# Last output tile in two column pieces, and split value and sum columns for eight attention pairs in place of four

## The chip, the cores and the metric

The kernel runs on one core of a Trainium2 chip. The metric is the device time of one execution in microseconds (us), given as the median of several executions. "The span" is the time from the first to the last instruction in one profiled execution; it lies some 1.7 us below the device time.

## The reference

Attention with a short "beacon" in front of the keys, causal, on 8 batches of 8 heads; then a dense MLP on its output.

```python
# q, k, v: (8, 8, 576, 64)   beacon_k, beacon_v: (8, 8, 16, 64)
k_all = concatenate([beacon_k, k], axis=2)
v_all = concatenate([beacon_v, v], axis=2)
scores = q @ k_all^T / sqrt(64);  scores[future keys] = -1e9
a = exp(scores - max);  a /= a.sum(-1) + 1e-9
x = (a @ v_all) as (4608 tokens, 512)
h = x @ w_in                                  # 512 -> 2048
out = (h * sigmoid(1.702 h)) @ w_out          # 2048 -> 512, float32
```

## The kernel before

The attention is done in 32 steps; a step is a "pair" of heads of one batch. TensorE makes the scores, ACT their exponentials, GpSimd and DVE the causal mask, and then TensorE multiplies the exponentials by an array that holds the values and, beside them, columns of a constant; those columns give the sums by which the values are divided. Tokens of finished pairs go through the MLP in nine groups of 512, whose matmuls are threaded between the pairs. So TensorE nearly always has work.

There are two forms for values and sums. The **old form** makes one tile per head and half, with the values on 64 partitions and the sums on the other 64. It is evicted from PSUM to an SBUF tile `O`, and all later work reads that copy:

```python
def av_half(i, x, half):                       # head x of pair i: 7 matmuls for two halves
    u = psu.tile([P, AQ[half + 1] - AQ[half]], F32, tag="u", name="u")
    ...
        nc.tensor.matmul(u[:, lo:hi], vb[...128 columns: values and constant...], E[0:kw, x, ...], ...)
def av_out(i, x, half, eng):                   # eviction, on DVE or ACT
    copy[eng](out=Os[i][:, x, AQ[half] : AQ[half + 1]], in_=avu[(i, x, half)][:, :])
def z_turn(i, x):                              # sums: transpose 32x32 squares
    nc.vector.transpose(zst[i][0][64*x : 64*x+64, :, :], Os[i][64*(1-x) : 64*(1-x)+64, x, :])
# z_recip: 1/sum;  z_back: transpose back;
def norm(i, x, eng):                           # values * 1/sum, 64 partitions
    vec[eng].tensor_tensor(out=xT[r : r+64, ...], in0=Os[i][r : r+64, x, :], in1=zst[i][2][r : r+64, :], op=ALU.mult)
```

The **split form** sends values (z = 0) and sums (z = 1) of both heads to tiles of their own, with the two heads side by side in two 64-column parts of the array. Both are read straight from PSUM; the pair's two sum tiles are made first, then its two value tiles:

```python
def av_both(i, half, z):                       # 32 matmuls a pair
    u = psu.tile([P, AQC[half + 1] - AQC[half]], F32, tag="u", name="u")
    ...
            for x in range(2):
                nc.tensor.matmul(u[64*x : 64*x+64, lo:hi], vb[0:kw, j, 2*p + x, z*D : (z+1)*D], Es[i][0:kw, x, ...], ...)
def z_turn_both(i, half):
    nc.vector.transpose(zst[i][0][:, ...], avu[(i, half, 1)][:, :])
def norm_both(i, half):
    nc.vector.tensor_tensor(out=xT[:, p, ...], in0=avu[(i, half, 0)][:, :], in1=zst[i][2][:, qa:qe], op=ALU.mult)
```

All these tiles, and those of the MLP, come from one ring of four PSUM buffers called "u" (`rings = dict(..., u=4, ...)`). The second layer of the MLP and its store:

```python
def mlp2(g, mt):                               # 16 matmuls of 512 columns
    o = psu.tile([P, DMODEL], F32, tag="u", name="u")
    for nt in range(NNT):
        nc.tensor.matmul(o[:, :], gts[g][:, nt, mt*P : (mt+1)*P], w2t[:, nt, :], ...)
def mlp2_out(g, mt, eng): ...                  # copy o to SBUF "osb" on DVE or ACT
def mlp2_store(g, mt):
    nc.sync.dma_start(out=out[t0 : t0 + P, :], in_=ou[(g, mt)][:, :])
```

The order of all instructions is chosen while the program is built, by a list scheduler in the kernel. Every piece of work has a duration (the "price"), things it needs, and perhaps a buffer. The scheduler takes the piece that can start first by its own clock, and emits it. Each engine then runs its own list in order, waiting where it must.

```python
while todo:
    for w in todo:
        t = 0.0
        for n in w.needs: ...; t = max(t, n.t1 + SEM)         # everything it needs is done
        if w.alloc is not None: ...                            # the buffer's former users are done
        eng = min(w.opts, key=lambda e: max(t, free[e]) + w.opts[e] + BIAS[t > 45].get(e, 0))
        c = (t, 0 if w.mode == mode == 1 else 1, w.key)
        ...                                                    # the smallest c wins
    w.t0 = t; w.t1 = t + d; free[eng] = t + d
    if w.dma:
        if eng == "POOL":                                      # loads that GpSimd issues
            f = max(dma_free["POOL"], t + d + 1.6) + w.dma
            w.t1 = f + (0.4 if t < 40 else 1.0)                # believed landing
```

The softmax here doesn't subtract the row's maximum and nothing guards it: scores larger than these inputs give would overflow.

Of the kernel before, what the change touches and what calls it, by code (L numbers as in the profile page):

```python
# [10 lines left out]
F32 = mybir.dt.float32  # L11
# [5 lines left out]
def kernel(  # L17
# [11 lines left out]
    nc = tc.nc  # L29
# [5 lines left out]
    DMODEL = H * D  # L35
    DFF = moe_w_in.shape[1]
    P = 128
# [5 lines left out]
    NNT = DFF // P  # L43
# [8 lines left out]
    GT = 512  # L52
    NG = NTOK // GT
# [15 lines left out]
    sp = ctx.enter_context(tc.tile_pool(name="sp", bufs=3))  # L69
    pss = ctx.enter_context(tc.tile_pool(name="pss", bufs=2, space=bass.MemoryType.PSUM))  # L70
    psu = ctx.enter_context(tc.tile_pool(name="psu", bufs=4, space=bass.MemoryType.PSUM))
    dr = ctx.enter_context(tc.tile_pool(name="dr", bufs=4, space=bass.MemoryType.DRAM))

    copy = dict(ACT=nc.scalar.copy, DVE=nc.vector.tensor_copy, POOL=nc.gpsimd.tensor_copy)
# [20 lines left out]
    w2t = cst.tile([P, NNT, DMODEL], F16, tag="w2", name="w2")  # L95
# [435 lines left out]

    ou = {}

    def mlp2(g, mt):
        o = psu.tile([P, DMODEL], F32, tag="u", name="u")
        ou[(g, mt)] = o
        for nt in range(NNT):
            nc.tensor.matmul(  # L538
                o[:, :],
                gts[g][:, nt, mt * P : (mt + 1) * P],  # L540
                w2t[:, nt, :],
                start=(nt == 0),
                stop=(nt == NNT - 1),
            )

    def mlp2_out(g, mt, eng):
        osb = sp.tile([P, DMODEL], F32, tag="osb", name="osb")
        if eng == "ACT":
            nc.scalar.copy(out=osb[:, :], in_=ou[(g, mt)][:, :])
        else:  # L550
            nc.vector.tensor_copy(out=osb[:, :], in_=ou[(g, mt)][:, :])  # L551
        ou[(g, mt)] = osb

    def mlp2_store(g, mt):
        t0 = g * GT + mt * P
        nc.sync.dma_start(out=out[t0 : t0 + P, :], in_=ou[(g, mt)][:, :])



# [21 lines left out]
    )  # L581
    SEM, QS = 0.1, 0.1
    SPL, CAP = 2.0, 2.0
    NBOTH = 4
    HWQ = 3

    def use(buf, *ws):
# [3 lines left out]
    Lq, V, W1, W2 = {}, {}, [], []  # L591
# [81 lines left out]
    for b in range(B):  # L673
# [5 lines left out]
        for g in range(2) if b >= NB2 else ():  # L679
            for w in (1, 0):  # L680
                k0 = 4 * b + 2 * g - 2.5 + 0.2 * (1 - w)
# [3 lines left out]
                    dma=1.4,  # L685
# [12 lines left out]
                for e in range(2):  # L698
# [3 lines left out]
                        tr, alloc=tb_ if e == 0 else None, after=cp[:1],  # L702
# [3 lines left out]
                if w == 1:  # L706
                    if bkB is None:
# [3 lines left out]
                                alloc=stb["bk"] if x == 0 else None, dma=0.2,  # L711
# [9 lines left out]
                        bkB, after=cp[:1],  # L721
# [4 lines left out]
                    dma=0.9,  # L726
# [4 lines left out]
                    alloc=bt[w] if g == 0 else None, dma=1.2,  # L731
                    after=[placed[(b, 0, w)]] if g == 1 else (),
# [4 lines left out]
        for j in range(NJ):  # L737
            V[(b, j)] = Work(
                "POOL", 0.88 + 0.54 * (j == 0), kv + 0.1 * j, lambda b=b, j=j: load_v(b, j),
                alloc=vbb[b] if j == 0 else None, after=[V[(b, 0)]] if j else (),  # L740
                dma=1.1 + 0.1 * (j == 0),
            )
    for c in range(4):
# [3 lines left out]
            after=[Lq[(2, 1, 0)]],  # L747
# [20 lines left out]
    for i in range(NSTEP):  # L768
# [5 lines left out]
        for c in range(len(CH)):  # L774
# [6 lines left out]
                alloc=s_, mode=1,  # L781
# [8 lines left out]
                alloc=Eb if c == 0 else None,  # L790
                after=[first] if first else exps[i - 1][:1] if i else (),
# [16 lines left out]
        if i < NBOTH:  # L808
            for z in (1, 0):
                for half in range(2):  # L810
# [8 lines left out]
                        after=avs[-1:],  # L819
# [5 lines left out]
                    if z == 1:  # L825
# [3 lines left out]
                            alloc=zb[0] if not zn else None, after=zn[:1],  # L829
                        ))  # L830
                        use(ub[(half, 1)], zn[-1])
        else:
            Ob = Buf("O")
            evs = []
            for x in range(2):
                for half in range(2):
                    mm = av_list(x, half)
                    u_ = Buf("u")
# [14 lines left out]
                        alloc=Ob if not evs else None, after=evs[:1],  # L853
# [4 lines left out]
                    alloc=zb[0] if not zn else None, after=zn[:1],  # L858
# [5 lines left out]
        if i < NBOTH:  # L864
            for half in range(2):
# [3 lines left out]
                    after=[norms[b * NPAIR][0]] if p + half else (),  # L869
# [27 lines left out]
    m1s, m2s = {}, {}  # L897
    for g in range(NG):
        gb[g] = Buf("g")
        bs = range(g * GT // S, ((g + 1) * GT - 1) // S + 1)  # L900
        gl = []
        k0 = ends[g] - 1 + 2 * max(0, g - 7)
        for n in range(NNT):
            u_ = Buf("u")
            m = Work(
                "PE", 0.88, k0 + 0.05 * n, lambda g=g, n=n: mlp1(g, n),
                [x for b in bs for p in range(NPAIR) for x in norms[b * NPAIR + p]] + [W1[n // 4]],
                alloc=u_,
            )
            m1s.setdefault(g, []).append(m)  # L910
            for b in bs:
                use(xTb[b], m)
            gl.append(Work(
                "ACT", 0.6 + (LOAD if n == 0 else 0), k0 + 0.05 * n - 0.3,
                lambda g=g, n=n: mlp1_gelu(g, n), [m], alloc=gb[g] if n == 0 else None,
                after=gl[:1] if n else exps[ends[g] - 1] + prev,
            ))
            use(u_, gl[-1])
        if ends[g] < NSTEP:
            x = exps[ends[g]][0]  # L920
            x.opts = dict(ACT=x.opts["ACT"] + LOAD)
            x.after += gl
        prev = gl
        for n in range(GT // P):
            u_, o_ = Buf("u"), Buf("osb")
            k1 = k0 + 1 + n
            m = Work("PE", 3.46, k1, lambda g=g, n=n: mlp2(g, n), gl + W2, alloc=u_)
            m2s[(g, n)] = m
            use(gb[g], m)
            oc = Work(  # L930
                dict(ACT=0.6, DVE=0.66), 0, k1 - 0.3, lambda eng, g=g, n=n: mlp2_out(g, n, eng),
                [m], alloc=o_,
            )
            use(u_, oc)
            ot = Work("SP", 0.73, k1, lambda g=g, n=n: mlp2_store(g, n), [oc], dma=0.9)
            use(o_, ot)


# [139 lines left out]
```

## Time and profile before

| | before |
|---|---|
| device time, median of 3 runs | 367.96 us (367.85 to 367.99) |
| span of the profiled run | 366.9 us (that execution took 368.57 us) |
| busy: PE, DVE, ACT, POOL (GpSimd) | 353.5, 249.3, 228.0, 153.1 us |
| first matmul of MLP group 0 | 35.54 us |
| starts of group 0's output tiles | 59.42, 65.91, 71.95, 77.95 us |
| last matmul's end, last copy's start | 363.18, 363.20 us |

TensorE (PE) is busy for 96% of the span, so what counts is where it waits. In the timelines a row is: start, length, engine, line of the kernel, operation, out<-in, shapes, how many instructions, and in brackets the idle time before the row with what ended it. A row without brackets followed what was before it closely.

### The profile page before, as it was taken

Reading aid. Unit: us, or ns where it says so; the run is one execution under the profiler, and the core shown is the slowest. Engines: PE = TensorE matmul, PEld = TensorE weight load, DVE = VectorE, ACT = ScalarE, POOL = GpSimd, SP = SyncE. Lnnn points to the kernel's source line nnn. Section 1 sums busy time; section 2 is a strip of 40 time slices with the busy share of each in tenths; the row PEclk is TensorE's granted clock in tenths of the full one; section 3 lists DMA queues with packets and bytes.
Section 4 is the critical chain, followed back from the end, with each engine's and each line's share of the span. In section 5 each row is a group of like instructions: output and inputs, shape, how many; then the busy total and the mean of one; then the engine's idle time right before and its main releaser. Section 6 shows DMA issues by size and latency. Waiting matters only on the chain.

```text
span 366.9 us, 6133 instructions
## 1 busy us (share of the span) xinstructions
PE 353.5 (96%) x2349; PEld 176.8 (48%) x2349; DVE 249.3 (68%) x421; ACT 228.0 (62%) x335; POOL 153.1 (42%) x264
## 2 busy tenths in 40 slices
PE   7689999999999999999999999999999999999995
PEld 3355444444444444544445864544444454444442
DVE  5547499999999986999599949981995183010021
ACT  4669787648765776677857675677658734616200
POOL 9678567593368245743376236710430010000000
PEclk9969999999999999999999999999999999999999
DMA  9999999994689645894479537921100011000012
GB/s 143 148 206 189 188 237 234 220 113 100 191 235 175 129 130 145 129 171 132 126 111 142 164 112 144 134 88 32 59 30 29 2 57 57 2 29 29 30 57 86
DMA packets 69788, 43.41 MB, mean 118 GB/s; under 512 B 42624, under 2 KB 62080, under 8 KB 69760
## 3 DMA queue, kind: packets, MB, share of 16 engines
q0 software_dynamic: 49152, 18.19, 48.6%
q1 hardware_dynamic: 20400, 24.55, 21.2%
q8 instruction: 18, 0.29, 0.3%
q10 hardware_dynamic: 208, 0.29, 0.3%
q14 instruction: 10, 0.08, 0.1%
HBM read 44.60 MB, written 16.61 MB: 167 GB/s over the span
## 4 chain that ended last, share of the span: by engine, by line
PE 79%; DVE 11%; DMA 3%; ACT 3%; POOL 2%; issue 1%; DVEq 0%; POOLq 0%
PE u L516 34%; PE u L538 30%; PE u L401 7%; PE s L331 6%; DMA g<-in_q_dram 3%; ACT E L344 2%; DVE zt L470 2%; DVE O L459 2%; DVE xT L489 2%; DVE t L262 1%; PE u L430 1%; POOL vb L221 1%; DVE rz L480 1%; DVE osb L551 1%; PE u L190 1%
## 5 line engine op out<-in xcount | busy, mean ns | idle before, releaser
L344 ACT ACTIVATE E<-s 128x1024 f16<-128x1024 f32 (+3 forms) x128 | 103.4, 865 | 48.7 <-PE s L331 46.5
L538 PE MATMUL u<-w,g 128*128 128x512 f16 x576 | 129.2, 379 | 0.6 <-DVE O L459 0.4
L516 PE MATMUL u<-xT,w 128*128 128x512 f16 (+1 forms) x640 | 126.0, 358 | 0.0
L528 ACT ACTIVATE g<-u 128x512 f16<-128x512 f32 x144 | 85.2, 597 | 42.8 <-PE u L516 42.5
L367 POOL TENSOR_SCALAR_AFFINE_SELECT E<-E 128x256 f16<-128x256 f16 (+2 forms) x148 | 63.8, 450 | 83.8 <-ACT E L344 83.6
L516 PEld LDWEIGHTS <-w 128*128 128x128 f16 x640 | 62.1, 98 | 61.3 <-issue 0.9
L538 PEld LDWEIGHTS <-g 128*128 128x128 f16 x576 | 54.5, 98 | 65.4 <-issue 3.6
L551 DVE COPY osb<-u 128x512 f32<-128x512 f32 x30 | 20.5, 683 | 65.2 <-PE u L538 65.0
L459 DVE COPY O<-u 128x240 f32<-128x240 f32 (+1 forms) x84 | 34.8, 440 | 24.4 <-PE u L401 22.1
L262 POOL COPY t<-sq 128x576 f16<-128x576 f16 x21 | 26.7, 1274 | 49.2 <-DVE sq L253 42.8
L401 PE MATMUL u<-E,vb 128*128 128x240 f16 x392 | 46.8, 266 | 0.2
L489 DVE TENSOR_TENSOR xT<-O,rz 64x576 f16<-64x576 f32 x56 | 44.3, 790 | 0.8
L470 DVE STREAM_TRANSPOSE zt<-O 64x576 f32<-64x576 f32 x56 | 43.1, 770 | 1.4
L401 PEld LDWEIGHTS <-vb 128*128 128x128 f16 x392 | 32.2, 98 | 17.4 <-issue 8.0
L331 PE MATMUL s<-qT,kT 64*128 64x80 f16 (+5 forms) x384 | 37.1, 285 | 2.8 <-ACT E L344 1.8
L253 DVE STREAM_TRANSPOSE sq<-n 128x576 f16<-128x576 f16 x48 | 34.9, 747 | 6.6 <-DMA n<-in_k_dram 6.3
L221 POOL DMA_DIRECT2D vb<-in_v_dram x40 | 34.4, 866 | 3.6 <-DMA w<-in_moe_w_in_dram 2.6
L262 DVE COPY t<-sq 128x576 f16<-128x576 f16 x27 | 27.6, 1021 | 0.3
L331 PEld LDWEIGHTS <-kT 64*128 64x128 f16 x384 | 13.3, 94 | 27.4 <-issue 19.4
L480 DVE STREAM_TRANSPOSE rz<-rt 128x576 f32<-128x576 f32 x32 | 24.4, 763 | 0.6
L459 ACT COPY O<-u 128x336 f32<-128x336 f32 (+1 forms) x28 | 10.7, 428 | 2.9 <-PE u L401 2.7
L1043 PE MATMUL u<-wu 128*128 128x512 f16 x29 | 10.5, 456 | 1.3 <-DVE wu L1036 1.3
(44 smaller groups left out, 124.5 us busy)
## 6 DMA issues: line engine op xcount, KB each, us to landing
out_dram<-osb SPq DMA_DIRECT2D x36, 256.0 KB, 2.1
d<-t SPq DMA_DIRECT2D x12, 296.0 KB, 2.6
kT<-d SPq DMA_DIRECT2D x12, 296.0 KB, 3.4
n<-in_k_dram POOLq DMA_DIRECT2D x12, 288.0 KB, 4.8
n<-in_q_dram POOLq DMA_DIRECT2D x12, 288.0 KB, 5.9
d<-t SPq DMA_DIRECT2D x12, 288.0 KB, 2.4
qT<-d SPq DMA_DIRECT2D x12, 288.0 KB, 3.2
vb<-in_v_dram POOLq DMA_DIRECT2D x24, 128.0 KB, 5.7
```

The lines of the kernel that those rows point to most:

```text
L221: nc.gpsimd.dma_start(out=vb[r : r + hi - lo, j, :, 0:D], in_=v[b, :, lo:hi, :].rearrange("h n d -> n h d"),)
L262: copy[eng](out=tqk[(b, g, w)][:, e, o : o + S].rearrange("p (r t) -> p r t", t=TPP), in_=sqs[(b, g, w)][:, :, e, :].rearrange("p t r -> p ...
L331: nc.tensor.matmul(sc[:, x, o : o + e - a], kT[r : r + 64, p, j * P : (j + 1) * P], qT[r : r + 64, p, a:e], start=True, stop=True,)
L344: nc.scalar.activation(out=Es[i][:, :, choff[ci] : choff[ci] + w], in_=scs[(i, ci)][:, :, 0:w], func=AFT.Exp, scale=0.125,)
L367: nc.gpsimd.affine_select(out=blk, in_=blk, compare_op=ALU.is_ge, fill=0.0, base=mc, pattern=[[0, 2], [1, w]], channel_multiplier=-1,)
L401: nc.tensor.matmul(u[:, lo:hi], vb[0:kw, j, :, :].rearrange("r h c -> r (h c)")[:, o : o + 2 * D], E[0:kw, x, col : col + hi - lo], start= ...
L459: copy[eng](out=Os[i][:, x, AQ[half] : AQ[half + 1]], in_=avu[(i, x, half)][:, :])
L470: nc.vector.transpose(zst[i][0][64 * x : 64 * x + 64, :, :], Os[i][64 * (1 - x) : 64 * (1 - x) + 64, x, :])
L489: vec[eng].tensor_tensor(out=xT[r : r + 64, p, c : c + S], in0=Os[i][r : r + 64, x, :], in1=zst[i][2][r : r + 64, :], op=ALU.mult,)
L516: nc.tensor.matmul(u[:, o : o + w], w1t[:, kp, nt * P : (nt + 1) * P], xT[:, kp, m : m + w], start=(kp == 0), stop=(kp == NKP - 1),)
L528: nc.scalar.activation(out=gts[g][:, nt, :], in_=hu[(g, nt)][:, :], func=AFT.Gelu_apprx_sigmoid)
L538: nc.tensor.matmul(o[:, :], gts[g][:, nt, mt * P : (mt + 1) * P], w2t[:, nt, :], start=(nt == 0), stop=(nt == NNT - 1),)
```

## The change

It has two aims. Pairs 4 to 7 take the split form as pairs 0 to 3 do, which saves DVE its evictions. And the very last output tile is made in two pieces of 384 and 128 columns, so that only a small copy and a small store stand behind the last matmul. The copies of the two pieces may go to DVE only.

```diff
+    TAIL = (0, 384, DMODEL)
-    def mlp2(g, mt):
-        o = psu.tile([P, DMODEL], F32, tag="u", name="u")
+    def mlp2(g, mt, a=0, e=DMODEL):
+        o = psu.tile([P, e - a], F32, tag="u", name="u")
 ...
-                w2t[:, nt, :],
+                w2t[:, nt, a:e],
 ...                      # mlp2_out and mlp2_store take a and e in the same way
-    NBOTH = 4
+    NBOTH = 8
 ...
-        for n in range(GT // P):
+        for n, a, e in [
+            (n, a, e)
+            for n in range(GT // P)
+            for a, e in (zip(TAIL, TAIL[1:]) if (g, n) == (NG - 1, GT // P - 1) else [(0, DMODEL)])
+        ]:
 ...
-            m = Work("PE", 3.46, k1, lambda g=g, n=n: mlp2(g, n), gl + W2, alloc=u_)
+            m = Work(
+                "PE", NNT * (e - a) / 2370, k1, lambda g=g, n=n, a=a, e=e: mlp2(g, n, a, e),
+                gl + W2, alloc=u_, after=[m2s[(g, n)]] if a else (),
+            )
```

More of the change, by code (lines that the diff above doesn't have):

```diff
@@ L532 @@
     ou = {}
-    def mlp2(g, mt):
-        o = psu.tile([P, DMODEL], F32, tag="u", name="u")
-        ou[(g, mt)] = o
+    TAIL = (0, 384, DMODEL)
+    def mlp2(g, mt, a=0, e=DMODEL):
+        o = psu.tile([P, e - a], F32, tag="u", name="u")
+        ou[(g, mt, a)] = o
         for nt in range(NNT):
@@ L544, in mlp2, with mlp2_out, mlp2_store @@
             )
-    def mlp2_out(g, mt, eng):
-        osb = sp.tile([P, DMODEL], F32, tag="osb", name="osb")
-        if eng == "ACT":
-            nc.scalar.copy(out=osb[:, :], in_=ou[(g, mt)][:, :])
-        else:
-            nc.vector.tensor_copy(out=osb[:, :], in_=ou[(g, mt)][:, :])
-        ou[(g, mt)] = osb
-    def mlp2_store(g, mt):
+    def mlp2_out(g, mt, eng, a=0, e=DMODEL):
+        osb = sp.tile([P, e - a], F32, tag="osb", name="osb")
+        copy[eng](out=osb[:, :], in_=ou[(g, mt, a)][:, :])
+        ou[(g, mt, a)] = osb
+    def mlp2_store(g, mt, a=0, e=DMODEL):
         t0 = g * GT + mt * P
-        nc.sync.dma_start(out=out[t0 : t0 + P, :], in_=ou[(g, mt)][:, :])
+        nc.sync.dma_start(out=out[t0 : t0 + P, a:e], in_=ou[(g, mt, a)][:, :])
     class Work:
@@ L923 @@
         prev = gl
-        for n in range(GT // P):
-            u_, o_ = Buf("u"), Buf("osb")
-            k1 = k0 + 1 + n
-            m = Work("PE", 3.46, k1, lambda g=g, n=n: mlp2(g, n), gl + W2, alloc=u_)
+        for n, a, e in [
[3 more added lines that the diff above has]
+        ]:
+            u_, o_ = Buf("u"), Buf("osb")
+            k1 = k0 + 1 + n + 0.1 * (a > 0)
+            m = Work(
+                "PE", NNT * (e - a) / 2370, k1, lambda g=g, n=n, a=a, e=e: mlp2(g, n, a, e),
+                gl + W2, alloc=u_, after=[m2s[(g, n)]] if a else (),
+            )
             m2s[(g, n)] = m
@@ L930 @@
             oc = Work(
-                dict(ACT=0.6, DVE=0.66), 0, k1 - 0.3, lambda eng, g=g, n=n: mlp2_out(g, n, eng),
-                [m], alloc=o_,
+                dict(ACT=0.6, DVE=0.66) if e - a == DMODEL else dict(DVE=0.66), 0, k1 - 0.3,
+                lambda eng, g=g, n=n, a=a, e=e: mlp2_out(g, n, eng, a, e), [m], alloc=o_,
             )
             use(u_, oc)
-            ot = Work("SP", 0.73, k1, lambda g=g, n=n: mlp2_store(g, n), [oc], dma=0.9)
+            ot = Work(
+                "SP", 0.73, k1, lambda g=g, n=n, a=a, e=e: mlp2_store(g, n, a, e), [oc], dma=0.9
+            )
             use(o_, ot)
```

## The prediction

> **What bounds the kernel now.** I read the page first for the shares, then the busy time by stretches for the stage in which pairs 4 to 7 run, then the chain of waits and the timeline for what holds TensorE there and at the end, and last the groups by shape for the price of each instruction.
>
> The page says that TensorE is the bound nearly everywhere: 96% busy, and the chain that ended last is 79% PE. In the second row the busy tenths of DVE are high only up to slice 16.
>
> ```profile
> PE   7689999999999999999999999999999999999995
> DVE  5547499999999986999599949981995183010021
> 49.40:65.90 16.50, 15.41 (x146) 8.09 (x146) 15.66 (x31) 13.02 (x19) 12.27 (x20) 1.00 1.50 232
> 65.90:84.00 18.10, 18.09 (x127) 8.95 (x127) 17.60 (x33) 10.77 (x18) 13.77 (x23) 1.00 1.10 155
> ```
>
> The last two lines are stretches (start:end in us, length, busy us of PE, PEld, DVE, ACT, POOL, clock, DMA share, GB/s). Pairs 4 to 7 live in them: DVE is 95% and 97% busy, but PE shows 15.41 of 16.50 and then 18.09 of 18.10. So DVE time saved after 65.9 cannot shorten anything at that place. The open question is 49.4 to 65.9, where part of the PE time is filler (L1043 multiplies zeros to keep the clock up):
>
> ```profile
> 50.18 1.28 ACT L344 ACT_TABLE_LOAD   x1
> 51.47 3.13 ACT L344 ACTIVATE E<-s 128x1024 f16<-128x1024 f32 x4
> 54.46 0.67 ACT L198 COPY qT<-u 128x576 f16<-128x576 f16 x1
> 54.98 3.19 ACT L344 ACTIVATE E<-s 128x1024 f16<-128x1024 f32 x4
> 52.55 0.37 PE L331 MATMUL s<-qT,kT 64*128 64x464 f16 x2 [0.68 <-ACT E L344]
> 54.97 1.42 PE L1043 MATMUL u<-wu 128*128 128x512 f16 x5
> 57.16 0.26 PE L331 MATMUL s<-qT,kT 64*128 64x208 f16 x2
> 63.37 1.87 PE L401 MATMUL u<-E,vb 128*128 128x240 f16 x14
> 65.17 0.60 PE L331 MATMUL s<-qT,kT 64*128 64x512 f16 x8
> 65.91 0.38 PE L538 MATMUL u<-w,g 128*128 128x512 f16 x1
> ```
>
> From 50.18 to 58.17 ACT works without a gap: table load, four exponentials of pair 5, one copy of a transposed q, four exponentials of pair 6. There are only two score buffers, so the score matmul of 57.16 waits for the second exponential of pair 6. TensorE had useful work for only part of these 8 us; nine fillers (x1, x1, x5 and x2; about 0.216 us each from 3.46 us for 16, so 1.9 us) and about 1.0 us of waiting stand in it. That slack belongs to ACT's exponentials, not to the DVE work which the change removes. After 57.2 DVE does cost something: the 14 matmuls at 63.37 take 1.80 us to the next start where the same 14 take 1.53 us when undisturbed, and 0.2 us passes between the end of the eight score matmuls (0.53 us after 65.17) and the matmul of 65.91. Together about 0.5 us, both waits for one of the four "u" buffers in PSUM, which late DVE copies hold.
>
> The end of the kernel:
>
> ```profile
> 342.44 20.73 PE u L538 x96
> 363.18 0.02 issue
> 363.20 0.69 DVE osb L551
> 363.92 0.33 SPq L556 DMA_DIRECT2D out_dram<-osb  x1
> 364.75:365.00 0.25, 0.00 (x0) 0.00 (x0) 0.00 (x0) 0.00 (x0) 0.00 (x0) 1.00 0.90 344
> 365.25:365.50 0.25, 0.00 (x0) 0.00 (x0) 0.00 (x0) 0.00 (x0) 0.00 (x0) 1.00 0.83 311
> ```
>
> Six tiles of 16 matmuls in one unbroken row, then one after the other a copy of 512 columns (0.69), the issue at 363.92, packets from 364.75 to about 365.47 (0.72 us of movement), and some 1.4 us until the span ends at 366.9. All of that is exposed.
>
> **What the Trainium skill says.** "TensorEngine Tiling (Array Packing)", section "PSUM Bottleneck": tiling speeds up TensorE but not the evacuation of PSUM. Here it is the other way about: the split form leaves TensorE's time as it was and saves evacuation, because the two heads' values land on their final partitions. "Perfetto Trace Analysis", section "Optimizing Scalar/DVE Operations": a fixed cost of about 125 ns for DVE on PSUM. The copies of this trace agree: 396, 496 and 683 ns for 240, 336 and 512 columns lie near 143 ns plus 1.055 ns a column. "TensorE: Matmul & The Clock Gate", section "Back-to-back issue gap": 128 columns take about 56 ns alone but about 81 ns in a stream of weight loads and matmuls. This trace gives the former, below. "DMA: Bandwidth & Descriptors", section "Specifications": at least 512 B a transfer for line rate; the small piece has rows of exactly 512 B, and no transfer of this trace shows that shape being written to the output.
>
> **The change, part by part.** The groups that the two forms cost (mean ns after the comma):
>
> ```profile
> L459 DVE COPY O<-u 128x240 f32<-128x240 f32 x47 | 18.6, 396 | 22.4 <-PE u L401 22.1
> L470 DVE STREAM_TRANSPOSE zt<-O 64x576 f32<-64x576 f32 x56 | 43.1, 770 | 1.4
> L441 DVE STREAM_TRANSPOSE zt<-u 128x320 f32<-128x320 f32 x4 | 2.1, 518 | 0.9 <-PE u L430 0.6
> L449 DVE TENSOR_TENSOR xT<-u,rz 128x320 f16<-128x320 f32 x4 | 1.9, 484 | 0.2 <-PE u L430 0.2
> ```
>
> *Evacuation of pairs 4 to 7.* Old form of a pair: four evictions, 2 x 0.396 + 2 x 0.496 = 1.78; two transposes of the sums, 1.54; reciprocal 0.25; transpose back 0.76; two multiplications of 0.79, 1.58; sum 5.91 us. Split form, from the rows of pairs 0 to 3: transposes 0.450 + 0.518, reciprocal 0.25, back 0.76, multiplications 0.425 + 0.484; sum 2.89. That is 3.0 us a pair and 12 us in all, of which ACT did four of the sixteen evictions (about 1.4 us by its own rows), so some 10 us leave DVE. Nearly all of it lies beside TensorE's work. On the path lie the 0.5 us at 63 to 66, which I count as recovered.
>
> *ACT.* With DVE freer near 51 to 54 the kernel's own list scheduler (it chooses the engine of each flexible copy as the program is built) may give the third q or k copy to DVE. Without it the exponentials of pair 6 start at 54.60 in place of 54.98: 0.38 us. I give it half: 0.2.
>
> *TensorE.* The split form has 32 matmuls in place of 14. By starts, pair 2 takes 1.60 us for its 32 and pair 5 takes 1.53 for its 14, so +0.07 a pair; for pairs 6 and 7 it lies on the path, for 4 and 5 partly in the slack: -0.2 us of gain.
>
> *The last tile.* From 7 matmuls with 1664 columns in 0.71 us and 16 with 8192 columns in 3.46 us: 0.4186 ns a column and 2 ns a matmul. So 384 columns take 0.163 us, sixteen 2.60; 128 columns 0.056, sixteen 0.89; together 3.49, or +0.03. The copy and the store of the large piece end beside the small piece: copy 0.143 + 384 x 1.055 ns = 0.55, from about 362.3; packets from about 363.75 to 364.3. The small piece is copied in 0.143 + 0.135 = 0.28 in place of 0.69: -0.41. A quarter of the bytes at the same rate would move in 0.18 us; I take 0.27 for short rows, so -0.45. Its packets start near 364.37, after the first piece's. Sum: +0.03 - 0.41 - 0.45 = -0.83 us.
>
> Total: 367.96 - 0.5 - 0.2 + 0.2 - 0.83 = 366.6 us, rounded.
>
> **The rivals.** *PSUM becomes the wait.* A split pair's two value tiles stay in their "u" buffers until transposes, reciprocal, transpose back and multiplication are done, some 2.9 us of DVE time, while an evicted tile is free after 0.5. With four buffers, six allocations of TensorE later this would stall pairs 5 to 7 by up to 1 us each, time about 369. For it: DVE is 95% busy and has other work between. Against it: a 3.46 us output tile stands between two pairs, pairs come every 6.0 us, and the load itself falls by half. *The freed DVE time reaches the path later.* Later DVE waits of the "u" buffer are worth about 0.5 us near 116 and 0.2 us at each of three group ends; if the lag clears, 365.5. Against it: DVE stood idle 0.56 us shortly before the wait near 116, so its order and not its load made that wait. *The scheduler shuffles.* Every flexible copy is placed anew from the first changed pair on; any such change can open or close waits of 0.2 to 0.6 us on TensorE. This goes either way and is most of my width. *The small piece doesn't stream.* At 81 ns a matmul it takes 1.30 us, and the tail gains only 0.4; at the same landing time as the large store, the same again.
>
> **Range and chances.** The tail is the surest term, 0.4 to 1.0. The middle lies between a gain of 1.3 and a loss of 0.9. Added, 8 times in 10 the time is between 365.4 and 367.6. A change of 2% is 7.4 us; the slack of TensorE after 49 us, fillers included, is about 5 us beyond the mode switches, so faster by 2% needs more than there is, and slower by 2% needs a stall of nearly 2 us at every changed pair.
>
> **What would show it.** Right: DVE falls from 249 to near 239 us; the fillers near 55 stay (about 1.9 us); the output matmul of 65.91 starts 0.4 to 0.9 us earlier; the last copy takes 0.28 us and the span from the last matmul's end to the end falls from 3.7 to about 2.8. Wrong: a wait of TensorE on a multiplication of the split form, a shift at 84 us of more than 1 us either way, or a small piece of over 1.1 us on TensorE.

## More of the kernel before

From batch 2 on, q and k are loaded by GpSimd's queue, and DVE turns their 32x32 squares (`tr_squares`, two halves of a tile); then comes a copy that puts them in order (`tr_order`, on DVE or GpSimd). This work needs a landed load and nothing of TensorE.

## The result, and the profile after

The changed kernel took 368.63 us (median of 6 runs, 367.96 to 368.97); the kernel before, beside it, 367.98 (6 runs, 367.39 to 368.43). A ratio here is the mean time of one kernel's fast runs over that of the other's of the same rounds, so not quite the ratio of the medians: 1.0014, with a 95% interval of 1.0001 to 1.0028. The class is "same", as predicted, but the time is above the range of 365.4 to 367.6, and the change, meant to save 1.4 us, cost about half a microsecond.

The busy tenths of TensorE and DVE, and the two stretches, in the same views as shown of before:

```profile
PE   7688999899999999999999999999999999999996
DVE  5556595699969977999599959981896173010021
49.40:65.90 16.50, 15.79 (x194) 8.60 (x189) 11.38 (x27) 12.31 (x16) 11.48 (x21) 1.00 1.55 226
65.90:84.00 18.10, 16.31 (x130) 8.30 (x129) 14.34 (x32) 8.85 (x12) 12.13 (x20) 1.00 1.09 194
```

DVE has its free time: 11.38 and 14.34 us busy in place of 15.66 and 17.60, and 239.3 in the whole, as predicted. But in the second stretch TensorE works for 16.31 us in place of 18.09. It has lost what it never lost before. The groups of the page say on what (the first number is busy time, the last the idle time before the group):

```profile
L541 PE MATMUL u<-w,g 128*128 128x512 f16 (+2 forms) x592 | 129.3, 374 | 1.8 <-DVE zt L441 1.8
```

The output tiles waited for 1.8 us in all, and all of it for one transpose of sums (L441). TensorE's timeline shows where:

```profile
54.12 1.47 PE L1052 MATMUL u<-wu 128*128 128x512 f16 x5
...
64.23 0.60 PE L331 MATMUL s<-qT,kT 64*128 64x512 f16 x8
64.76 3.63 PE L541 MATMUL u<-w,g 128*128 128x512 f16 x16
...
70.31 0.60 PE L331 MATMUL s<-qT,kT 64*128 64x512 f16 x8
72.69 3.61 PE L541 MATMUL u<-w,g 128*128 128x512 f16 x16 [1.79 <-DVE zt L441]
```

The fillers (L1052 now) are still there. The second output tile follows its score matmuls at once (64.23 + 0.53, then 64.76), so the wait of before at that place is gone. The third starts at 72.69 when it could have started at 70.84. Pair 7's four tiles fill all four "u" buffers, and the output tile needs the first of them, that of the sums; so it waits until DVE has turned those sums. Why DVE was late is to be seen in its own timeline. Of the kernel before:

```profile
71.49 1.24 DVE L459 COPY O<-u 128x240 f32<-128x240 f32 x3
72.64 1.57 DVE L470 STREAM_TRANSPOSE zt<-O 64x576 f32<-64x576 f32 x2
...
74.78 0.72 DVE L253 STREAM_TRANSPOSE sq<-n 128x576 f16<-128x576 f16 x1
```

Of the changed kernel, with one line of its chain of waits at the end (start, length, what):

```profile
65.33 0.82 DVE L449 TENSOR_TENSOR xT<-u,rz 128x256 f16<-128x256 f32 x2
69.10 1.44 DVE L253 STREAM_TRANSPOSE sq<-n 128x576 f16<-128x576 f16 x2 [2.94 <-DMA n<-in_k_dram]
70.98 0.78 DVE L253 STREAM_TRANSPOSE sq<-n 128x576 f16<-128x576 f16 x1 [0.44 <-DMA n<-in_q_dram]
71.68 0.60 DVE L262 COPY t<-sq 128x576 f16<-128x576 f16 x1
72.20 0.83 DVE L441 STREAM_TRANSPOSE zt<-u 128x256 f32<-128x256 f32 x2
...
59.89 10.99 DMA n<-in_q_dram
```

Before, DVE was so far behind that pair 7's work came first and the first square transposes of batch 3 (L253) only at 74.78. After, DVE is done with pair 6 at 66.1, and next in its list stand three square transposes and a copy. Their loads have not landed. DVE sits idle for 2.94 and again 0.44 us, with pair 7's sums behind it in the list. The last load was issued at 59.89 and landed 10.99 us later. (From 55 to 75 us the packets of GpSimd's queue alone took 99.5% of the time of the 16 DMA engines.) DVE isn't slow here, nor is it busy: it is waiting, in order, for a DMA.

What the scheduler believed about it, from its own list as the program is built:

```
                                  scheduler   chip
k load (batch 3, first half) in       67.0    69.1
q load (batch 3, first half) in       68.4    70.9
first square transpose of k           67.1    69.10
transposes of pair 7's sums           70.15   72.20
```

By its clock nothing waits: the loads are in by 68.4 and DVE has finished with them by 70.15, just as the sums come. Its TensorE times agree with the trace to about 0.4 us up to pair 7's first sums (it has them start at 69.04, the trace at 68.70); its landings are 2.1 and 2.5 us early.

The end of the kernel, from the chain, DVE's timeline and the stretches:

```profile
342.80 20.77 PE u L541 x112
...
362.70 0.56 DVE L551 COPY osb<-u 128x384 f32<-128x384 f32 x1 [1.91 <-PE u L541]
363.60 0.29 DVE L551 COPY osb<-u 128x128 f32<-128x128 f32 x1 [0.34 <-PE u L541]
...
364.75:365.00 0.25, 0.00 (x0) 0.00 (x0) 0.00 (x0) 0.00 (x0) 0.00 (x0) 1.00 0.78 230
365.00:365.25 0.25, 0.00 (x0) 0.00 (x0) 0.00 (x0) 0.00 (x0) 0.00 (x0) 1.00 0.13 33
```

The matmuls take 20.77 us (before 20.73), the last copy 0.29 (before 0.69), and the packets end soon after 365.0, some 0.4 us earlier than before. But the span ends at 366.9 in both. From the start of the last copy to the end of the span it is 3.65 us before and 3.34 after. The records of SyncE's semaphore waits show what lies between:

```
                                      before    after
last copy starts                     363.20    363.60
last store issued                    363.92    363.92
its semaphore's wait passed          365.95    365.60
further closing waits, 0.061 us each      -    seven
last closing wait passed             365.95    366.03
span ends                            366.85    366.94
```

At the end SyncE passes nine closing waits in a fixed order, each for one or two semaphores. The stores of the output take their semaphores from a rotation of eight. With one store more, the last one has moved from the semaphore that stands last in that order to one that stands second. The waits behind it are long fulfilled, but SyncE passes them only afterwards: 7 x 0.061 = 0.43 us.

**The sum by stages.** MLP group 0 starts at 35.54 before and at 34.66 after. That isn't the change: up to there the two programs are the same, and over the runs, that start lies anywhere between 34.66 and 35.83. So I count from it. To the end of group 0's first layer: the same 13.92. To the first output tile: +0.14 (10.10 in place of 9.96). To the second: -0.41. To the third: +1.89. To the fourth and the next group: +0.14. From there to the last matmul: -0.49, with the wait near 116 us of before gone. After it: -0.30. The sum is +0.97 us. The span of the profiled run doesn't show it, since the early start hides it.

### The profile page after: what moved, and what is told of

Read it like the earlier page. It is cut to its first block, busy times and chain, and to the rows that moved or that the text cites. A ratio compares the mean times of both kernels' runs of the same rounds, so it can differ in the third digit from the quotient of the medians.

```text
span 366.9 us, 6295 instructions
## 1 busy us (share of the span) xinstructions
PE 352.4 (96%) x2438; PEld 178.3 (49%) x2438; DVE 239.3 (65%) x413; ACT 227.4 (62%) x331; POOL 150.2 (41%) x261
## 4 chain that ended last, share of the span: by engine, by line
PE 75%; DMA 17%; DVE 3%; POOL 2%; issue 1%; ACT 1%; POOLq 0%; DVEq 0%
PE u L541 31%; PE u L516 30%; PE u L401 8%; PE s L331 5%; DMA vb<-in_v_dram 5%; DMA w<-in_moe_w_out_dram 5%; DMA w<-in_moe_w_in_dram 4%; DMA n<-in_q_dram 3%; ACT E L344 1%; DVE t L262 1%; POOL vb L221 1%; DVE O L459 1%; DVE zt L470 1%; DVE xT L489 0%; POOL g L146 0%
## 5 line engine op out<-in xcount | busy, mean ns | idle before, releaser
L541 PE MATMUL u<-w,g 128*128 128x512 f16 (+2 forms) x592 | 129.3, 374 | 1.8 <-DVE zt L441 1.8
L367 POOL TENSOR_SCALAR_AFFINE_SELECT E<-E 128x256 f16<-128x256 f16 (+2 forms) x146 | 61.1, 439 | 85.6 <-ACT E L344 85.5
L551 DVE COPY osb<-u 128x512 f32<-128x512 f32 (+2 forms) x30 | 20.0, 665 | 69.0 <-PE u L541 69.0
L459 DVE COPY O<-u 128x240 f32<-128x240 f32 (+1 forms) x73 | 30.4, 440 | 25.9 <-PE u L401 23.3
L253 DVE STREAM_TRANSPOSE sq<-n 128x576 f16<-128x576 f16 x48 | 34.9, 748 | 10.2 <-DMA n<-in_k_dram 9.4
L401 PE MATMUL u<-E,vb 128*128 128x336 f16 (+4 forms) x336 | 40.2, 266 | 0.1
L470 DVE STREAM_TRANSPOSE zt<-O 64x576 f32<-64x576 f32 x48 | 37.0, 770 | 1.2
L489 DVE TENSOR_TENSOR xT<-O,rz 64x576 f16<-64x576 f32 x48 | 37.1, 774 | 0.7
L401 PEld LDWEIGHTS <-vb 128*128 128x128 f16 (+1 forms) x336 | 27.8, 97 | 15.2 <-issue 7.0
L430 PE MATMUL u<-E,vb 128*64 128x320 f16 (+5 forms) x256 | 14.8, 259 | 2.1 <-POOL E L367 1.6
L430 PEld LDWEIGHTS <-vb 128*64 128x64 f16 (+1 forms) x256 | 11.5, 112 | 5.6 <-issue 2.9
```

Of the source, the lines that this page charges most:

```text
L253: nc.vector.transpose(sqs[(b, g, w)][:, c * n : (c + 1) * n, :, :], nat[(b, g, w)][:, c * n : (c + 1) * n, :],)
L367: nc.gpsimd.affine_select(out=blk, in_=blk, compare_op=ALU.is_ge, fill=0.0, base=mc, pattern=[[0, 2], [1, w]], channel_multiplier=-1,)
L401: nc.tensor.matmul(u[:, lo:hi], vb[0:kw, j, :, :].rearrange("r h c -> r (h c)")[:, o : o + 2 * D], E[0:kw, x, col : col + hi - lo], start= ...
L470: nc.vector.transpose(zst[i][0][64 * x : 64 * x + 64, :, :], Os[i][64 * (1 - x) : 64 * (1 - x) + 64, x, :])
L489: vec[eng].tensor_tensor(out=xT[r : r + 64, p, c : c + S], in0=Os[i][r : r + 64, x, :], in1=zst[i][2][r : r + 64, :], op=ALU.mult,)
L541: nc.tensor.matmul(o[:, :], gts[g][:, nt, mt * P : (mt + 1) * P], w2t[:, nt, a:e], start=(nt == 0), stop=(nt == NNT - 1),)
```

## The experiments

Twelve kernels ran, all correct. The time of the kernel before in them was 368.43 (11 runs), 368.38 (12, of which 11 are those of the first call) and 368.32 (10). So e5 to e8 have a single execution of the kernel before from their own call, and it took 367.77 us: their ratios to it are less sure than the intervals say. "Stall" is the time between the last score matmul and the first matmul of the third output tile, from matmul starts (about 0.1 us of it is there without a stall too); "tail" is from the start of the last copy to the end of the span.

| run | median, us | ratio to before (95%) | stall | tail |
|---|---|---|---|---|
| before | 368.3 to 368.4 | | - | 3.65 |
| changed kernel | 368.63 | 1.0014 (1.0001 to 1.0028) | 1.95 | 3.34 |
| e1 tail alone | 368.12 | 0.9997 (0.9984 to 1.0010) | none | 3.34 |
| e2 pairs alone | 370.39 | 1.0063 (1.0049 to 1.0077) | 1.94 | 3.65 |
| e3 order mended | 367.96 | 0.9987 (0.9975 to 0.9999) | < 0.1 | 3.34 |
| e4 small store by ACT | 368.37 | 1.0001 (0.9989 to 1.0014) | 0.81 | 3.38 |
| e5 one store by GpSimd | 367.57 | 0.9979 (0.9964 to 0.9993) | 1.42 | 2.91 |
| e6 later landings believed | 369.79 | 1.0040 (1.0027 to 1.0053) | none | 3.34 |
| e7 pairs alone, same price | 368.74 | 1.0011 (0.9997 to 1.0026) | 1.16 | 3.65 |
| e8 = e3 + e5 | 366.78 | 0.9959 (0.9946 to 0.9972) | none | 2.91 |
| e9 changed kernel again | 368.60 | 1.0008 (0.9995 to 1.0021) | 2.39 | 3.35 |
| e10 tail alone + e5 | 367.88 | 0.9992 (0.9980 to 1.0005) | none | 2.90 |
| e11 e8, q load only | 367.20 | 0.9975 (0.9962 to 0.9987) | 1.10 + 0.44 | 2.91 |
| e12 later landings to 60 us + e5 | 366.13 | 0.9945 (0.9932 to 0.9958) | none | 2.90 |

**My theory** was that pair 7's sums wait behind loads in DVE's list (the stall), and that the small store's gain is eaten by its place among the closing waits. **The rivals:** the split form holds PSUM too long, so that the stall would stay whatever the order; and the small store is slow because its rows are short.

### e1: the tail alone

```diff
 # the changed kernel
-    NBOTH = 8
+    NBOTH = 4
```

> Only the last tile in two pieces; pairs 4 to 7 in the old form. The prediction's sum says -0.83 us against the kernel before. Theory 'closing waits' (SP passes its waits for the DMA semaphores one after the other at the end; the last store's semaphore is now an early one in that row, so some seven waits of 0.06 us follow it): -0.3 to -0.4 us, a span end some 1.8 us after the last packet in place of 1.4. Rival 'short rows are slow': the landing itself of the small store takes as long as that of the large one, about 2.0 us after its issue.

Measured: 368.12 us, ratio 0.9997. The tail is 3.34 in place of 3.65, so the half of the change that I thought surest gives about 0.3 us by the trace. The small store's wait is passed 1.69 us after its issue, as in the changed kernel, where 256 KB in one piece take 2.03: it isn't slower than the large store. The rows of 512 B are not what eats the gain. (By its packets it moves a little slower for its size; see the last section.)

### e2: the pairs alone

```diff
 # the kernel before
-    NBOTH = 4
+    NBOTH = 8
```

> Only the split form for pairs 4 to 7; last tile whole. The prediction says -0.5 us. Theory 'head of the DVE queue' (the scheduler now puts three transposes of the next k and q load ahead of pair 7's transposes of the sums, and that load lands late): the wait of TensorE before the third output tile of group 0 stays at 1.8 to 2.0 us, and the kernel is 0.8 to 1.4 us slower than before. Rival 'PSUM is held too long by the split form': the same time, so this run prices the part and does not tell the two apart.

Measured: 370.39 us, some 2 us over the kernel before, where 0.8 to 1.4 were expected, and worse than the two parts together. (The profiled execution, at 371.87, is the slowest of the six.) The stall is there (1.94), so it belongs to the pairs. But there is a second one of the same size, which the changed kernel doesn't have, ahead of a first-layer matmul. The lines of TensorE, DVE and GpSimd:

```profile
88.70 7.50 PE L516 MATMUL u<-xT,w 128*128 128x512 f16 x34 [1.77 <-DVE O L459]
...
84.15 4.06 DVE L489 TENSOR_TENSOR xT<-O,rz 64x576 f16<-64x576 f32 x2
...
85.32 1.16 POOL L262 COPY t<-sq 128x576 f16<-128x576 f16 x1
```

The two multiplications of 84.15 should take 1.5 us. The first took 3.29 us by itself, the second 0.755, the usual time. GpSimd ran a copy, a select, a copy and a select without a gap from 83.82 to 86.83, and the multiplication ended 0.62 us after that, which is about the time it needs alone. The Trainium skill, "SBUF — State Buffer", section "Who interferes with whom", says that a DVE instruction with two SBUF inputs contends with a GpSimd instruction that reads SBUF, that this contention is an exclusive lock, and that the order of issue decides who is blocked. The trace agrees, and shows more: it stayed blocked across four GpSimd instructions. The pattern is not this trace's alone: in nine places of six traces this multiplication, begun some 0.6 us into a GpSimd copy, took 1.65 us and ended 0.62 us after the copy (before: 128.98, copy from 128.39 to 130.01). Beside two selects and no copy it took 0.87 (before: 145.58). That it waited through four instructions is seen once, and no run varied this alone.

Why did the changed kernel not have it? The two schedules differ here only by the price of an output tile, 3.46 against 3.4565. Run e7 tests that.

### e3: pair 7's sums ahead of the square transposes

```diff
 # the changed kernel; sqw is a new dict, filled where the square transposes are made
+                sqw[(b, g, w)] = tr
 ...
+        if i == 7:
+            for w in (1, 0):
+                sqw[(3, 0, w)][0].after += zn      # zn: the transposes of the sums
```

> The whole change, with one ordering added: the DVE transposes of the k and q load of batch 3 (first half) may be put only after pair 7's transposes of the sums. Nothing else in what the split form holds is altered. Theory 'head of the DVE queue': the wait of 1.95 us before the output tile near 70 us goes to under 0.2, and the kernel is 1.5 to 2.1 us faster than the changed one, 0.6 to 1.4 us faster than the one before. Rival 'PSUM is held too long': TensorE still waits more than 1 us on a multiplication or transpose of a split pair, and the time is within 0.4 us of the changed kernel.

Measured: 367.96 us, ratio 0.9987. That is 0.5 us under the kernel before and 0.7 under the changed one, so the expectation for the time missed (0.6 to 1.4 and 1.5 to 2.1). TensorE's timeline:

```profile
70.62 0.60 PE L331 MATMUL s<-qT,kT 64*128 64x512 f16 x8
71.15 3.63 PE L541 MATMUL u<-w,g 128*128 128x512 f16 x16
```

The stall is gone with the same four buffers, the same split form, the same loads and the same list for TensorE. The rule did more than turn round two entries of DVE's list: from there the scheduler placed eight flexible pieces on other engines, the copy of the second output tile among them (from ACT to DVE). None of these works on a PSUM tile of a split pair, so the rival of PSUM held too long is refuted. A wait of 0.57 us opened at 81.95, ahead of a value matmul, so not all of the gain came out.

### e4: the small store issued by ACT

```diff
 # the changed kernel
-        nc.sync.dma_start(...)
+        (nc.scalar if a else nc.sync).dma_start(...)
```

> The whole change, with the store of the small piece issued from ScalarE's queue, so that its semaphore is another and, I believe, stands in the last of the closing waits. Theory 'closing waits': 0.3 to 0.5 us less than the changed kernel, with the span ending 1.3 to 1.5 us after the last packet. Rival 'short rows are slow': no change, within 0.15 us.

A miss that taught something. I expected that a store from ACT's queue would use a semaphore apart. It took the very one that it had before: stores of SyncE and ACT share one rotation. The small store's wait was passed 1.72 us after its issue and the same seven waits followed, so the run tested nothing about the tail. Its stall was 0.81 us, with a late start of the MLP (35.83).

### e5: another store issued by GpSimd

```diff
 # the changed kernel
-        nc.sync.dma_start(...)
+        (nc.gpsimd if (g, mt) == (NG - 1, 0) else nc.sync).dma_start(...)
```

> The whole change, with one earlier output store (first tile of the last group, 14 us before the end) issued from GpSimd's queue. The stores of the SP queue take eight semaphores in turn, so the small last store gets back the semaphore whose wait is the last of SP's closing waits. Theory 'closing waits': the wait that the small store ends is the last one, the span ends 1.4 us after the last packet in place of 1.85, and 0.35 to 0.5 us are saved against the changed kernel. Rival 'short rows are slow': unchanged within 0.15 us, by the stretch from the small piece's issue to the end.

This takes the first output tile of the last group out of the rotation, so that the last store's semaphore is again the last that is waited for. The tail is 2.91 us in place of 3.34: the 0.43 us of closing waits came off to the hundredth. The small store's wait was passed 1.69 us after its issue, and the span ended 0.9 us later, as in the kernel before. The time is 367.57, ratio 0.9979, with the stall still there (1.42). That is 1.0 us under the changed kernel, over twice what the tail explains and more than was expected; the kernel before, too, was fast in its one execution of that call (367.77), so the rest may lie between the calls. The trace is the firmer evidence here.

### e6: the scheduler believes later landings, everywhere

```diff
 # the changed kernel
-                    w.t1 = f + (0.4 if t < 40 else 1.0)
+                    w.t1 = f + (0.4 if t < 40 else 3.5)
```

> The whole change, with one number of the kernel's own scheduler changed: loads from GpSimd's queue are taken to land 2.5 us later after 40 us than it assumed, about what the trace of the changed kernel shows for the k and q load of batch 3. Theory 'head of the DVE queue, from a load thought too early': the scheduler itself puts pair 7's transposes of the sums first, and the wait near 70 us falls from 1.95 to under 0.3; time 0.8 to 1.8 us under the changed kernel, unless the new order makes other waits. Rival 'PSUM is held too long': a wait over 1 us before an output tile of group 0 remains.

Measured: 369.79 us, so the expectation for the time missed. Yet TensorE has no wait at all between 60 and 90 us, which is what the theory says of this place. The loss is elsewhere: four new waits, each right ahead of a later MLP group, at 121.5, 160.6, 199.8 and 239.3 us (0.97, 0.96, 1.19 and 0.75; together 3.9 us). One belief for all loads is right for one stage and, it seems, wrong for the next; e12 tests that.

### e7: the pairs alone, with the changed kernel's price

```diff
 # the kernel before
-    NBOTH = 4
+    NBOTH = 8
-            m = Work("PE", 3.46, k1, ...
+            m = Work("PE", NNT * DMODEL / 2370, k1, ...
```

> Only the split form for eight pairs, last tile whole, but with the output tile's price in the scheduler as the changed kernel has it (3.4565 in place of 3.46 us), so that the order of all engines is that of the changed kernel up to the last tile. Theory: the second wait of run 2, 1.94 us near 86.5, came of that 4 ns in the scheduler's sums and not of the split form; it is gone here, and the time is 0.2 to 0.5 us over the changed kernel, some 1.3 us under run 2. Rival: it belongs to the split form without the divided tile; the time stays near that of run 2.

Measured: 368.74 us, 1.65 under e2 where some 1.3 was expected. The second wait of e2 is gone, the stall is 1.16, the tail 3.65. So 4 ns in a price that only the scheduler reads moved the time by 1.6 us (370.39 against 368.74), and e2 was no clean test of the pairs. This one is: with the tail of before, the pairs cost about 0.4 us (ratio 1.0011, and its interval holds 1; from the start of MLP group 0 the traces show 331.73 us against 331.31).

### e8: order mended, and one store by GpSimd

The edits of e3 and e5 together.

> The ordering of run 3 and the store of run 5 together: if the two causes are separate they add, so 0.35 to 0.5 us under run 3 and 0.6 to 1.1 us under the kernel before. If the order of the closing waits is not a cause, the same as run 3.

Measured: 366.78 us, ratio 0.9959, without the stall and with a tail of 2.91. With both faults mended the change gains: 1.6 us by this ratio, but 1.0 against the one execution of the kernel before. Against e3 it is 1.2 us, where 0.35 to 0.5 were expected; the tail explains 0.43 of that, and e3 ran in another call. From the start of MLP group 0 the trace shows 330.18 us, against 331.31 before: 1.1 us.

### e9: the changed kernel once more

No edit.

> The changed kernel itself once more, so that it shares its runs of the kernel before with the runs beside it. Both theories: 0.3 to 0.9 us over the kernel before; the output tile that waits near 70 starts at 72.5 to 73.0 us whatever the time at which the first MLP group starts, because the landing of the k and q load sets it.

Measured: 368.60 us, ratio 1.0008. In the profiled run, which at 370.98 is the slowest of its six (the others took 368.37 to 368.88), the third tile started at 73.46, so later than I expected, after a stall of 2.39. Here is that tile, and two stretches in it (columns as above; the clock is the third number from the end):

```profile
73.46 5.30 PE L541 MATMUL u<-w,g 128*128 128x512 f16 x16 [2.23 <-DVE zt L441]
...
75.00:76.00 1.00, 1.00 (x4) 0.30 (x2) 1.00 (x2) 0.00 (x0) 1.00 (x2) 0.50 0.84 281
76.00:77.00 1.00, 1.00 (x4) 0.33 (x3) 1.00 (x5) 0.00 (x0) 1.00 (x2) 0.50 0.03 9
```

The tile took 5.30 us in place of 3.6: after the wait the granted clock was halved, for some 3.4 us, and seven or eight of its matmuls took 0.43 us each in place of 0.216. The Trainium skill, "TensorE: Matmul & The Clock Gate", section "Why this matters for your kernels", advises no gaps of TensorE over about 3 us between bursts. In this run the clock fell 0.8 us after the end of a gap of 2.2 us, while after gaps of 1.8 us (the changed kernel's first profile, and e2) it stayed at 1.00. So this stall of some 2.3 us cost about 4 in all. A single profiled execution shows it; how often it happens I can't say, nor whether the length of the gap alone decides.

### e10: the tail alone, with one store by GpSimd

The edits of e1 and e5 together.

> Old form for pairs 4 to 7, last tile divided, and one earlier store from GpSimd's queue, so that the small store's wait is the last of the closing ones: the divided tile by itself without its side effect. Theory 'closing waits': 0.6 to 0.9 us under the kernel before, which is what the prediction had summed (0.83); from the last matmul's end to the end of the span 2.8 to 2.95 us in place of 3.3 in run 1. If only the copy is saved: 0.3.

Measured: 367.88 us, ratio 0.9992. By the trace the tail is 2.90, that is 0.75 us shorter than before and 0.4 shorter than e1. The timing shows 0.3 to 0.4 us, with an interval that reaches from -0.7 to +0.2, so the expectation for the time missed, while that for the tail came. The trace shows what the last steps take in one run; the median carries everything else, starts included.

### e11: only the q load's square transposes held back

```diff
 # e8
-            for w in (1, 0):
+            for w in (0,):
```

> As run 8, but only the transposes of the q load, not those of k, are held back until after pair 7's transposes of the sums. The k load lands near 69.1 us and its two transposes take 1.4, so theory 'head of the DVE queue' expects a wait of 0.1 to 0.6 us before the output tile near 71 in place of 1.95, and a time within 0.5 us of run 8.

Measured: 367.20 us, ratio 0.9975, 0.42 over e8. The wait before the output tile (0.44) and the time are as expected, but 1.5 us are lost in two places, and the other I had not foreseen. The k load, too, blocks DVE. The larger part is now a wait inside pair 7's value matmuls:

```profile
70.84 0.73 PE L430 MATMUL u<-E,vb 128*64 128x320 f16 x10 [0.94 <-DVE osb L551]
```

The copy of the second output tile (L551) stood behind the two transposes of k in DVE's list. It isn't one unlucky load, then: the k load, too, holds up what stands behind it in DVE's list.

### e12: later landings believed for loads of 40 to 60 us, and one store by GpSimd

```diff
 # the changed kernel, with e5's edit
-                    w.t1 = f + (0.4 if t < 40 else 1.0)
+                    w.t1 = f + (0.4 if t < 40 else 3.5 if t < 60 else 1.0)
```

> The later landing of run 6 given to the scheduler only for loads issued before 60 us by its own clock, so that the waits of about 1 us ahead of the later MLP groups in run 6 don't come; with the store of run 5. No wait over 0.3 us between 60 and 90; 0.2 to 0.6 us under run 8, the best of all, if later orders are no worse than in run 8.

Measured: 366.13 us (365.76 to 367.32), ratio 0.9945 (0.9932 to 0.9958): the best of all, and faster than both kernels, 2.2 us below the one before (ten executions). TensorE has no wait between 60 and 90 us, as expected. Its third tile follows at once:

```profile
71.97 3.63 PE L541 MATMUL u<-w,g 128*128 128x512 f16 x16
```

Its score matmuls started at 71.44 (71.44 + 0.53 = 71.97). With the belief corrected where the trace says it is wrong, and left alone elsewhere, the scheduler finds by itself an order without the stall, at least as good as the one I forced in e8 (366.78; the two intervals overlap). From the start of MLP group 0, the trace of this run shows 329.8 us to the end of the span, against 331.3 before: 1.5 us of the 2.2. The rest I can't place; the profiled run was the slowest of its six.

**How the stall depends on the run.** Its end is set by when the q load lands, not by TensorE. In four runs in which DVE's list is the same at this place, the third tile starts at nearly one time, however early TensorE came:

| run | MLP group 0 starts | third output tile starts | stall |
|---|---|---|---|
| changed kernel | 34.66 | 72.69 | 1.95 |
| e5 | 35.16 | 72.67 | 1.42 |
| e7 | 35.44 | 72.69 | 1.16 |
| e4 | 35.83 | 72.72 | 0.81 |

An early start is lost again at the load. This fits the medians, which show a loss of about 0.5 us where the profiled run, with its early start, shows 0.97 from that start on. (In e2 and e9 the third tile came later, at 73.74 and 73.46; what made the load later there is open.)

## Why the prediction was wrong

Point by point, by its own steps.

- **What bounds the kernel; the slack at 49 to 58.** Right, but for one reading that bears on nothing else: DVE's row is not high "only up to slice 16"; it has nines as late as slices 29 and 30. TensorE bounds it, and the fillers stayed although DVE was freed: that slack is ACT's.
- **Evacuation of pairs 4 to 7, some 10 us off DVE.** Right: 249.3 to 239.3.
- **"On the path lie the 0.5 us at 63 to 66, which I count as recovered."** Right as it stands: 0.41 us came.
- **ACT, 0.2.** Didn't come. One copy of a transposed q stayed on ACT between the exponentials of pairs 5 and 6, so these start 3.52 us apart (54.11 less 50.59) as before.
- **TensorE, +0.07 a pair.** Right: +0.14 to the first output tile.
- **The middle as a whole.** This is the step that failed, and the larger fault. The prediction took the free time of DVE as time that only shortens waits. It asked what DVE would finish sooner, and not what its list would start sooner. What moved up was work on loads, 2.1 to 2.5 us before these were in, and behind it the sums for which TensorE waited: a new wait of 0.8 to 2.4 us in the changed lists, against a gain of 0.4. From the start of the MLP to the last matmul the profiled run lost 1.2 us where the sum had a gain of 0.5. The rival "the scheduler shuffles" named the kind of thing, with waits of 0.2 to 0.6 us; so the range was too narrow by the size of one wait for a load. It was narrower than its own terms, too: a middle that loses 0.9 and a tail that gains 0.4 add to 368.5, and the range ended at 367.6. Loads on GpSimd's queue weren't looked at, though the trace of before showed that they take up to 11.0 us at that place (6.2 to 11.0 from 40 to 80 us).
- **The rival "PSUM becomes the wait".** Wrong, though near. The wait is for a "u" buffer, but not because the split form holds it for 2.9 us; in e3 it is held in the same way, and TensorE loses under 0.1.
- **The rival "the freed DVE time reaches the path later".** Partly right: after 84 us TensorE gained 0.49 us, and the wait near 116 is gone. Whether by load or by order isn't settled.
- **The last tile on TensorE, +0.03, and its copy, -0.41.** Right: +0.04 and -0.40. The pieces' copies take 0.56 and 0.29 us (0.55 and 0.28 predicted). The rival of 81 ns a matmul is refuted: 20.77 us for six tiles, the small piece included, leaves no room for it. (The fixed cost of a copy that the prediction fitted, 143 ns, is near the page's 125 and not equal to it.)
- **The last store, -0.45.** The mechanism was right, the size was off, and a term was missing. From issue to passed wait it is 1.69 us in place of 2.03, so -0.34. The movement itself shrank as forecast: by the packet records it takes 0.36 us (364.76 to 365.12) in place of 0.83 (364.75 to 365.58). But from the last packet's end to the passed wait it is 0.48 in place of 0.37. The missing term is +0.43 for the seven closing waits. Together: -0.40 - 0.34 + 0.43 = -0.31 from the last copy's start on, and with the +0.04 some -0.3 in place of -0.83. With the semaphores back in order (e10) it is -0.75 + 0.04, near the prediction.

Of what the prediction listed as signs, it got DVE's busy time, the fillers and the last copy right. The output tile of 65.91 came 1.15 us earlier by the clock, but 0.88 of that was the early start. And "a shift at 84 us of more than 1 us either way" is just what happened, counted from the start of the MLP: 1.76 us (0.88 by the clock).

## What to carry to other kernels

Where an engine works through a list in order, ask of freed time what moves up in its list and what that waits for: work moved ahead of a load that is not in blocks everything behind it. Compare the landings that a schedule assumes with those in the trace, stage by stage, and keep the schedule's other numbers fixed when parts of a change are tested apart, since 4 ns in a price moved 1.6 us here. At the end of a kernel, look at what is waited for after the last packet, and in which order.

## What the Trainium skill lacked or had wrong

- "TensorE: Matmul & The Clock Gate", section "Why this matters for your kernels": it advises against gaps over about 3 us. In e9 the clock was halved for some 3.4 us after a gap of 2.2 us, once; after gaps of 1.8 us it was not. In section "Back-to-back issue gap" the 81 ns for 128 columns in a stream of weight loads did not appear: the starts of the small piece's sixteen matmuls, each with its own weights, lie 56 ns apart in the changed kernel's trace (362.50 to 363.34).
- "SBUF — State Buffer", section "Who interferes with whom": it gives the block as lasting for the whole instruction of the one that issued first (said of another kind of DVE instruction). In e2 a DVE multiplication with two SBUF inputs took 3.29 us in place of 0.755 beside four GpSimd instructions without a gap, so the loser seems to stay blocked through all of them. That it is held to the end of one GpSimd copy is seen in nine places of six traces (1.65 us); that it is held through several, only here. Nor does the section say that GpSimd's instructions differ in this: beside two selects the multiplication took 0.87.
- "DMA: Bandwidth & Descriptors", section "Specifications": it gives 512 B as the smallest size for line rate. In the last stores a packet of 512 B took 26.9 ns and one of 2 KB 85.3 (means of 128), 19 and 24 bytes per ns, so at 512 B the rate was a fifth lower; over 8 packets an engine that is some 0.05 us. In all, 64 KB took 1.69 us from issue to passed wait and 256 KB took 2.03.
- I found on no page: that stores issued by SyncE and by ACT share one rotation of eight semaphores (e4 and e5), and that the closing waits behind the last store's own cost 0.061 us each, 0.43 us for seven.
- I found on no page: how long a load on GpSimd's queue takes when the queue is full; "DMA: Bandwidth & Descriptors" has a fit for a single transfer only. Here it was 10.99 us from issue to landing at 59.89 us, for 288 KB.
